# Group 1's first MLP product in seven half-size products, its weight sums read where GpSimd writes them

## The chip, the core and the metric

The kernel runs on one core of a Trainium2 chip. Five engines work side by side, each through its own instructions in order: TensorE (PE in the profile; PEld is its weight load), VectorE (DVE), ScalarE (ACT), GpSimd (POOL) and SyncE (SP), which here only issues DMAs. They wait for one another through semaphores. The metric is the device time of one execution in microseconds. All data are float32.

## The reference

Eight batches of 576 tokens go through chunked attention (8 heads of 64, chunks of 64 tokens), then a real two-dimensional Fourier mix over tokens and channels, a normalization, and an MLP with a residual. What matters here is the MLP, 512 to 2048 to 512:

```python
u = x + mixed
un = (u - mu) / np.sqrt(var + 1e-06)
ch = np.maximum(un @ w_ch1, 0.0) @ w_ch2
return (u + ch)
```

## The kernel before

**Groups.** Tokens are handled in tiles of 128. A tile LO or HI holds two chunks of one batch; a tile RE (rest) holds the middle chunks of two batches. Batch b's four LO and HI tiles are MLP group b (512 tokens), and the four rests are group 8: nine groups. `mlp(g)` (L1403) is a generator that issues the first product ("up") and the second ("down") of one group, and yields after each small piece.

**The step counter t.** The loop at L1484 counts these yields: t. After each, it issues side work: attention and Fourier mix of the next batch (`side`, spread evenly between due times `ready_at`), the preparation of the weights, and prefetches. So the order on every engine's queue is the order in which the program says it. `begin[g]` is the t at which group g starts; `begin[1]` is 32. Each up takes 16 steps; a down of group 0 takes 16, too, one for each m (128 of the 2048 hidden channels).

**Two forms of a product.** The plain form of up, `up_plain` (L1189), does for each m four matmuls of 128x128 weights by 512 tokens, and one ReLU by ScalarE from PSUM. In the profile each float32 matmul is two records. The other form, `up_halves` (L1245), splits weights, tokens and channels in halves and uses seven products of half size in place of eight (the Strassen-Winograd scheme). It goes over four pairs of m; a pair has seven turns, in the order `UP`, with four matmuls of 256 columns in each (r = 0, 1; kk = 0, 1). Its operands on the token side are the quarters of `unT`, the normalized and transposed tokens, and three sums of them, t1, t2, t4, with one quarter replaced, all made by `combined(g, q_)` (L1009) on VectorE. Its operands on the weight side are quarters of w_ch1 and four sums of them. The products gather in two PSUM tiles for each r, `pa` and `pb`, which take all four buffers of `ps_f`. Between products ScalarE copies one (L1267), VectorE adds five times for each m (L1268, L1270, L1272, L1278, L1281), and ScalarE applies the ReLU (L1276, L1279, L1282). A PSUM half is written again only after these have read it.

**Which group has which form.** `first_of = {1: 2, 2: 1}`: up is plain for groups 0 and 1, in halves from group 2; down is plain for group 0, in halves from group 1 (`down_halves`, L1291). For the last group down has a third form.

**Weights.** `wa` holds w_ch1 (`w1`), `wb` holds w_ch2 (`w2`). While group 0 runs, all weight pieces are rounded into place. `keep2` (GpSimd) makes the sums for down and SP stores them to DRAM (`s2`); this ends at t=31. `keep1` makes the sums for up during group 1, in four parts: GpSimd writes the sums to `yall` and to `os_` (the end of `wb`), and SP stores seven blocks for each part to DRAM (`s1`), 28 stores of 256 KB in all, in bunches of seven. Once `w1` is no more needed, `wa` becomes ten slabs that `fetch(1)` fills from `s1`; `wb` becomes three slabs of 1 MB that `fetch(2)` fills from `s2`, all three issued at t = begin[1] + 8.

**Around the start of group 1.** In the last steps of group 0's down, `turned(1, j)` (L997) transposes tile j on TensorE after m = 11 to 14, ScalarE copies the result to `unT` (L1007). After m=15, VectorE adds the residual to the four outputs (L1229) and the stores of group 0 go to SP and ScalarE (L1027, L1036). Beside it the attention of batch 2 runs: for each tile SP loads q and k (L250) and v (L273), VectorE transposes q and k (L416; for LO tiles GpSimd then copies a column, L418), TensorE makes scores (L448), transposes (L397) and the product with v (L498). `xall` keeps the attention outputs, 12 rows for tiles that rotate, 4 for the rests. GpSimd moves single token rows between tiles (L555) and folds the tiles for the Fourier mix (L570 to L595).

Of the kernel before, what the change touches and what calls it, by code (L numbers as in the profile page):

```python
# [11 lines left out]
ALU = mybir.AluOpType  # L12
# [4 lines left out]
def kernel(  # L17
# [32 lines left out]
    nc = tc.nc  # L50
    B, H, S, D = q.shape
    DM = H * D
    DFF = w_ch1.shape[1]
# [4 lines left out]
    NP = B // 2  # L58
    NJ = H // 2
    KD = DM // 128  # L60
    KF = DFF // 128
# [33 lines left out]
    wb = const.tile([128, KF * DM], FP32, name="wb")  # L95
    w1 = wa.rearrange("p (k f) -> p k f", k=KD)
# [6 lines left out]
    NO, HF = 7, KF // 2  # L103
    UP = (1, 0, 2, 3, 4, 6, 5)
    s1 = dram.tile([HF // 2, NO, 128, 2 * 2 * 128], FP32, name="s1")
    s2 = dram.tile([NO, 128, HF * HM], FP32, name="s2")
    NS1, NS2, Z1, Z2 = 10, 3, 2 * 2 * 128, HF * HM
    slab1 = [wa[:, i * Z1:(i + 1) * Z1].rearrange("p (k r f) -> p k r f", r=2, k=2) for i in range(NS1)]
    slab2 = [wb[:, i * Z2:(i + 1) * Z2].rearrange("p (m e) -> p m e", m=HF) for i in range(NS2)]
    tt = wa[:, NS1 * Z1:NS1 * Z1 + 3 * 2 * 256].rearrange("p (o k t) -> p o k t", o=3, k=2)  # L110
    tmp = wa[:, NS1 * Z1 + 3 * 2 * 256:NS1 * Z1 + 3 * 2 * 256 + 4 * 256].rearrange("p (i j t) -> p i j t", i=2, j=2)
    xs = wb[:, NS2 * Z2:NS2 * Z2 + HF * 256].rearrange("p (m t) -> p m t", m=HF)
    os_ = xs.rearrange("p (a b) t -> p a (b t)", b=2)
    yall = const.tile([128, 4, 512], FP32, name="yall")
# [66 lines left out]
    NG = len(groups)  # L181
# [3 lines left out]
    NR = 3 * G  # L185
    xall = const.tile([128, NR + NP, XW], FP32, name="xall")
# [819 lines left out]
        else:  # L1006
            nc.scalar.copy(unT[:, :, s * 128:(s + 1) * 128], pt)  # L1007

    def combined(g, q_):  # L1009

        unT = unTs[g]
        cl, ch = slice(q_ * 128, (q_ + 1) * 128), slice(256 + q_ * 128, 256 + (q_ + 1) * 128)
        b11, b12, b21, b22 = unT[:, 0:2, cl], unT[:, 0:2, ch], unT[:, 2:4, cl], unT[:, 2:4, ch]
        t1, t2, t4 = (tt[:, o, :, cl] for o in range(3))
        nc.vector.tensor_tensor(out=t1, in0=b12, in1=b11, op=ALU.subtract)
        nc.vector.tensor_tensor(out=t2, in0=b22, in1=t1, op=ALU.subtract)
        nc.vector.tensor_tensor(out=b12, in0=b22, in1=b12, op=ALU.subtract)
        nc.vector.tensor_tensor(out=t4, in0=b21, in1=t2, op=ALU.subtract)

    def store(n, o):  # L1020

# [14 lines left out]
                    eng.dma_start(out=out[b, t0 + 1 - r:t0 + CH:2, :], in_=o[r0 + ODD * r:r0 + ODD * r + ODD])  # L1036


    def keep1(i):

        f, kk = divmod(i, 2)
        lo, hi = slice(f * 512, (f + 1) * 512), slice(DFF // 2 + f * 512, DFF // 2 + (f + 1) * 512)
        a11, a12, a21, a22 = w1[:, kk, lo], w1[:, 2 + kk, lo], w1[:, kk, hi], w1[:, 2 + kk, hi]
        o1, o2, o3, o4 = ((os_ if i % 2 else yall)[:, j] for j in range(4))
        for out_, in0, in1, op in (
            (o1, a21, a22, ALU.add), (o2, o1, a11, ALU.subtract),
            (o3, a11, a21, ALU.subtract), (o4, a12, o2, ALU.subtract),
        ):
            nc.gpsimd.tensor_tensor(out=out_, in0=in0, in1=in1, op=op)
            yield  # L1050
        to = s1.rearrange("a o p (k x) -> p a o k x", k=2)[:, 2 * f:2 * f + 2]
        for o, a in enumerate((a11, o2, o1, o3, a12, o4, a22)):
            nc.sync.dma_start(out=to[:, :, o, kk], in_=a.rearrange("p (a x) -> p a x", a=2))
        yield

    def keep2(i):

# [23 lines left out]
    def block_of(name):  # L1081

        if name[0] == "s":
            return s3[STORED.index(name)]
        o, k = (2, "dw".index(name)) if name in "dw" else ({"b1": 0, "b2": 0, "b3": 4 + "12".index(name[2]), "b4": 4 + "12".index(name[2])}[name[:2]], (int(name[1]) - 1) % 2)
        return s2[o, :, k * Z3:(k + 1) * Z3]
# [38 lines left out]
                    yield  # L1125

    FEW = NG - 1
    first_of = {1: 2, 2: 1}
    n_slab = {1: 0, 2: 0, 3: 0}

    def fetch(which):
        i = n_slab[which]
        if which == 1 and i < HF // 2 * NO * (NG - first_of[1]):
            pair, o = divmod(i % (HF // 2 * NO), NO)
            nc.sync.dma_start(out=slab1[i % NS1].rearrange("p k r f -> p (k r f)"), in_=s1[pair, UP[o]])
        elif which == 3 and i < NR2 * (NG - FEW):
            to = slab3[i % NS3].rearrange("p m e -> p (m e)")
            nc.sync.dma_start(out=to, in_=block_of(PRODUCTS[i % NR2][1]))
        elif which == 2 and i < NO * (FEW - first_of[2]):
            nc.sync.dma_start(out=slab2[i % NS2].rearrange("p m e -> p (m e)"), in_=s2[i % NO])  # L1140
        n_slab[which] = i + 1

    lo, hi = slice(0, 256), slice(256, 512)
# [99 lines left out]


    def up_halves(g):  # L1245
        unT = unTs.pop(g)
        h1 = one_p.tile([128, KF, G * 128], FP32, tag="big", name="h1")
        rhs = (unT[:, 0:2, lo], tt[:, 1], tt[:, 0], unT[:, 0:2, hi], unT[:, 2:4, lo], unT[:, 2:4, hi], tt[:, 2])
        for pair in range(HF // 2):
            pas, pbs = {}, {}  # L1250
            for turn_, o in enumerate(UP):
                w = slab1[((g - first_of[1]) * HF // 2 * NO + pair * NO + turn_) % NS1]
                for r in range(2):
                    m = 2 * pair + r
                    a, b = tmp[:, r, 0], tmp[:, r, 1]
                    if o == 0:
                        pas[r] = ps_f.tile([128, 2, 256], FP32, tag="ff", name="pa")
                    if o == 1:
                        pbs[r] = ps_f.tile([128, 2, 256], FP32, tag="ff", name="pb")
                    dst = (pas, pbs, pas, pbs, pas, pas, pbs)[o][r][:, (0, 0, 1, 1, 0, 1, 1)[o]]  # L1260
                    for kk in range(2):
                        nc.tensor.matmul(  # L1262
                            out=dst, lhsT=w[:, kk, r], rhs=rhs[o][:, kk],
                            start=(o in (0, 1) and kk == 0), stop=(kk == 1), skip_group_check=True,
                        )
                    if o == 0:
                        nc.scalar.copy(a, dst)  # L1267
                        nc.vector.tensor_tensor(out=b, in0=pbs[r][:, 0], in1=a, op=ALU.add)  # L1268
                    elif o == 2:
                        nc.vector.tensor_tensor(out=a, in0=dst, in1=b, op=ALU.add)  # L1270
                    elif o == 3:
                        nc.vector.tensor_tensor(out=h1[:, HF + m, hi], in0=dst, in1=a, op=ALU.add)  # L1272
                        if pair > 0 and g < FEW:
                            operands(h1, m - 2)
                    elif o == 4:
                        nc.scalar.activation(out=h1[:, m, lo], in_=dst, func=ACTF.Relu)  # L1276
                    elif o == 5:
                        nc.vector.tensor_tensor(out=h1[:, m, hi], in0=dst, in1=b, op=ALU.add)  # L1278
                        nc.scalar.activation(out=h1[:, m, hi], in_=h1[:, m, hi], func=ACTF.Relu)  # L1279
                    elif o == 6:  # L1280
                        nc.vector.tensor_tensor(out=h1[:, HF + m, lo], in0=dst, in1=b, op=ALU.add)  # L1281
                        nc.scalar.activation(out=h1[:, HF + m], in_=h1[:, HF + m], func=ACTF.Relu)  # L1282
                fetch(1)
                if pair == HF // 4 and turn_ > 0 and g >= FEW:
                    sums(h1, EARLY.split()[turn_ - 1:turn_])
                if turn_ in (1, 3, 5, 6):
                    yield h1
        for m in (HF - 2, HF - 1) if g < FEW else ():
            operands(h1, m)
# [119 lines left out]
    with tc.manual_schedule():  # L1409
# [60 lines left out]
        begin = [0]  # L1470
# [1 line left out]
            begin.append(begin[-1] + (KF if g < first_of[1] else 2 * HF) + (KF if g < first_of[2] else 2 * NO if g < FEW else NR2 // 2))  # L1472
        ready_at = [begin[g] + (2 * KF - 7 if g < first_of[2] else 2 * HF + 4) for g in range(NG)]
        conv2 = iter([step for i in range(HF // 2) for step in [keep2(i ^ 1)]])
        conv1 = iter([step for i in range(4) for step in [keep1(i)]])

        def chain(gens):
            for gen in gens:
                yield from gen

        n_whole, late, rest_ = 0, [], None
        conv2, conv1 = chain(conv2), chain(conv1)
        t = 0
        for g in range(NG):  # L1484
            for _ in mlp(g):
# [4 lines left out]
                late = []  # L1490
                if t == 8:
                    nc.scalar.copy(tk, early_tk[:, :, :, 0:NE])
                if cur < len(sides):
                    t0 = 3 if cur == 0 else ready_at[cur - 1]
                    t1 = ready_at[cur]
# [19 lines left out]
                if t == begin[1] - 1:  # L1515
                    for _ in conv2:
                        pass
                if t == ready_at[NG - 3]:
                    rest_ = make_rest()
                    next(rest_)  # L1520
# [5 lines left out]
                    slab3.extend(a.rearrange("p (m e) -> p m e", m=4) for a in more)  # L1526
                if begin[FEW] + 2 <= t < begin[FEW] + 2 + NS3:
                    fetch(3)
                if begin[1] <= t < begin[1] + KF // 2:
                    for _ in range(3):  # L1530
                        next(conv1, None)
                if t == begin[1] + KF // 2:
                    for _ in range(NS2):
                        fetch(2)
                if t == begin[1] + KF:
                    for _ in range(NS1):
                        fetch(1)
# [49 lines left out]
```

## Time and profile before

| | |
|---|---|
| median of 3 runs | 1076.75 us (1076.54 to 1077.28) |
| the profiled execution | 1076.13 us |
| its span, first to last instruction | 1074.1 us |
| granted TensorE clock, mean | 0.997 |
| instructions | 19924 |
| group 1 up, 16 m | 190.49 to 255.96 us |
| group 1 down | 255.96 to 314.17 us |
| group 2 up, 28 turns | 314.17 to 370.13 us |
| DMA engines busy, 190 to 255 us | 0.77, 243 GB/s |

The span is the part of the execution that the trace covers; some 2 us lie around it. Busy time of TensorE is modelled from the instructions, so a share near 1 says that it has no gaps and not that it works at its peak. A time of a record is longer than its pace, since records overlap: the pace is read from the chain of waits, where a piece of work counts until the next one takes over. In answers of the trace, a bracket behind an instruction tells how long its engine was idle before it and what ended that.

### The profile page before, as it was taken

Reading aid. Unit: us, or ns where it says so; the run is one execution under the profiler, and the core shown is the slowest. Engines: PE = TensorE matmul, PEld = TensorE weight load, DVE = VectorE, ACT = ScalarE, POOL = GpSimd, SP = SyncE. Lnnn points to the kernel's source line nnn. Section 1 sums busy time; section 2 is a strip of 40 time slices with the busy share of each in tenths; the row PEclk is TensorE's granted clock in tenths of the full one; section 3 lists DMA queues with packets and bytes.
Section 4 is the critical chain, followed back from the end, with each engine's and each line's share of the span. In section 5 each row is a group of like instructions: output and inputs, shape, how many; then the busy total and the mean of one; then the engine's idle time right before and its main releaser. Section 6 shows DMA issues by size and latency. Waiting matters only on the chain.

```text
span 1074.1 us, 19924 instructions
## 1 busy us (share of the span) xinstructions
PE 1052.4 (98%) x7402; PEld 838.0 (78%) x7402; DVE 586.5 (55%) x1271; ACT 310.6 (29%) x730; POOL 406.8 (38%) x531
## 2 busy tenths in 40 slices
PE   8899989999999999999999999999999999999997
PEld 6645444446888888888888888888888888888886
DVE  4798985324556455655565555745664535433331
ACT  4688563122113410323022312331134103101200
POOL 4310018483514240254124321525151726780281
PEclk9999999999999999999999999999999999999999
DMA  8677566598468635892678356954653659776763
GB/s 171 215 204 217 126 196 189 176 295 287 155 182 238 173 134 179 235 253 91 194 214 239 119 166 190 258 159 154 208 174 107 222 188 334 244 233 190 280 229 104
DMA packets 159293, 212.71 MB, mean 198 GB/s; under 512 B 69308, under 2 KB 106172, under 8 KB 152926
## 3 DMA queue, kind: packets, MB, share of 16 engines
q1 hardware_dynamic: 155548, 208.04, 62.6%
q10 hardware_dynamic: 3330, 2.76, 1.1%
q8 instruction: 59, 0.97, 0.4%
q0 software_dynamic: 320, 0.66, 0.3%
q14 instruction: 36, 0.29, 0.1%
HBM read 177.31 MB, written 34.08 MB: 197 GB/s over the span
## 4 chain that ended last, share of the span: by engine, by line
PE 82%; DMA 5%; DVE 5%; ACT 3%; SPq 3%; issue 1%; POOL 0%; DVEq 0%; ACTq 0%
PE pb L1313 18%; PE pa L1262 18%; PE pa L1313 14%; PE pb L1262 13%; PE dn L1377 4%; PE up L1195 4%; PE pt L397 2%; PE dn L1216 2%; DMA xall<-in_moe_w_ch_dram 2%; PE mix L838 2%; PE z L719 1%; PE xp L498 1%; PE sc L448 1%; SPq L263 1%; DMA out_dram<-o 1%
## 5 line engine op out<-in xcount | busy, mean ns | idle before, releaser
L1262 PE MATMUL pa<-unT,wa 128*128 128x256 f32 x672 | 160.0, 381 | 1.5 <-DVE wa L1270 1.5
L1262 PEld LDWEIGHTS pa<-unT,wa 128*128 128x128 f32 x672 | 126.3, 190 | 19.3 <-DVE wa L1270 2.0
L1262 PE MATMUL pb<-wa 128*128 128x256 f32 x448 | 106.6, 381 | 0.0
L1313 PE MATMUL pa<-wb,h 128*128 128x256 f32 x448 | 101.6, 380 | 0.0
L1313 PE MATMUL pb<-wb,h 128*128 128x256 f32 x448 | 100.8, 380 | 0.0
L1262 PEld LDWEIGHTS pb<-wa 128*128 128x128 f32 x448 | 84.4, 190 | 11.5
L1313 PEld LDWEIGHTS pa<-wb,h 128*128 128x128 f32 x448 | 83.9, 190 | 11.2
L1313 PEld LDWEIGHTS pb<-wb,h 128*128 128x128 f32 x448 | 84.1, 190 | 10.9
L1149 POOL TENSOR_TENSOR h<-h 128x256 f32<-128x256 f32 x56 | 47.7, 861 | 98.7 <-DVE wb L1147 95.4
L555 POOL COPY xall<-xall 1x512 f32<-1x512 f32 x28 | 17.8, 636 | 147.9 <-DVE xall L515 120.4
L1268 DVE TENSOR_TENSOR wa<-pb,wa 128x256 f32<-128x256 f32 x56 | 23.8, 424 | 69.9 <-ACT wa L1267 69.9
L1216 PE MATMUL dn<-wb,h 128*128 128x512 f32 x128 | 59.2, 611 | 0.0
L1195 PE MATMUL up<-unT,wa 128*128 128x512 f32 x128 | 56.8, 596 | 0.0
L1267 ACT COPY wa<-pa 128x256 f32<-128x256 f32 x56 | 20.9, 373 | 123.8 <-PE pa L1262 98.9
L1262 PE MATMUL pa<-wa 128*128 128x256 f32 x224 | 53.9, 383 | 0.0
L1262 PE MATMUL pb<-unT,wa 128*128 128x256 f32 x224 | 52.9, 379 | 0.0
L1313 PE MATMUL pb<-wb,yall 128*128 128x256 f32 x224 | 51.2, 382 | 0.0
L1313 PE MATMUL pb<-wb 128*128 128x256 f32 x224 | 50.7, 379 | 0.0
L1313 PE MATMUL pa<-wb,yall 128*128 128x256 f32 x224 | 50.5, 379 | 0.0
L1276 ACT ACTIVATE h<-pa 128x256 f32<-128x256 f32 x56 | 21.5, 384 | 99.3 <-PE pa L1262 98.3
L1175 PE MATMUL up<-unT,wa 128*128 128x512 f32 x108 | 49.4, 598 | 0.0
L855 POOL TENSOR_TENSOR xall<-y,xall 128x513 f32<-128x513 f32 x14 | 21.4, 1526 | 68.4 <-DVE y L849 68.4
(287 smaller groups left out, 1977.9 us busy)
## 6 DMA issues: line engine op xcount, KB each, us to landing
wb<-s SPq DMA_DIRECT2D x49, 1024.0 KB
wa<-s SPq DMA_DIRECT2D x196, 256.0 KB
xall<-in_moe_w_ch_dram SPq DMA_DIRECT2D x22, 512.0 KB
q<-in_q_dram SPq DMA_DIRECT2D x96, 112.0 KB
k<-in_k_dram SPq DMA_DIRECT2D x96, 112.0 KB
wb<-s SPq DMA_DIRECT2D x16, 512.0 KB
v<-in_v_dram SPq DMA_DIRECT2D x124, 64.0 KB
s<-part SPq DMA_DIRECT2D x30, 256.0 KB
```

The lines of the kernel that those rows point to most:

```text
L397: nc.tensor.transpose(pt[:, j, :], src(j), ident)
L838: nc.tensor.matmul(out=mix[:, cols], lhsT=zt[:, T], rhs=tab, start=(T == 0), stop=(T == 3), skip_group_check=True,)
L855: eng.tensor_tensor(out=x[:, 0:w], in0=y[:, 0:w], in1=x[:, 0:w], op=ALU.add)
L1149: nc.gpsimd.tensor_tensor(out=h1[:, m, hi], in0=h1[:, m, lo], in1=h1[:, m, hi], op=ALU.subtract)
L1175: nc.tensor.matmul(out=up, lhsT=w1[:, kk, m * 128:(m + 1) * 128], rhs=unT[:, kk], start=(kk == 0), stop=(kk == KD - 1), skip_group_check=True,
L1195: nc.tensor.matmul(out=up, lhsT=w1[:, kk, m * 128:(m + 1) * 128], rhs=unT[:, kk], start=(kk == 0), stop=(kk == KD - 1),)
L1216: nc.tensor.matmul(out=dn, lhsT=h1[:, m, s * 128:(s + 1) * 128], rhs=w2[:, m, :], start=(m == 0), stop=(m == KF - 1),)
L1262: nc.tensor.matmul(out=dst, lhsT=w[:, kk, r], rhs=rhs[o][:, kk], start=(o in (0, 1) and kk == 0), stop=(kk == 1), skip_group_check=True,)
L1268: nc.vector.tensor_tensor(out=b, in0=pbs[r][:, 0], in1=a, op=ALU.add)
L1276: nc.scalar.activation(out=h1[:, m, lo], in_=dst, func=ACTF.Relu)
L1313: nc.tensor.matmul(out=dst, lhsT=lhs[:, m], rhs=w[:, m], start=(o in (0, 2) and m == 0), stop=(m == HF - 1), skip_group_check=True,)
L1377: nc.tensor.matmul(out=dst, lhsT=lhs[:, m], rhs=w[:, m], start=(fresh and not half and m == 0), stop=(m == 3), skip_group_check=True,)
```

## The change

Group 1's up takes the form in halves. Its weights are not fetched from DRAM but read in place: quarters from `w1`, the sums where GpSimd writes them, which is now the front of `wb` (12 blocks of 512 columns, `made1`), but for one sum that replaces a quarter of `w1`. `keep1` makes the four sums of one whole pair at t = 31, 33, 35 and 37, without a DMA; the 28 stores follow one by one, two for each step from t=33 to 46 (`keep1_store`). The three slabs of `w2` are fetched at begin[1] + 9, + 13 and + 16, one each.

Group 1's t1, t2, t4 and the two temporaries of the recombination can't lie in `wa`, where `w1` still is. They go to rows of `xall`: t1 and t2 to the rests' last two rows, which are not yet filled, t4 and the temporaries to group 0's rows. Since group 0's outputs are added from these rows, t4 is made later: `combined(1, q_)` without it runs in the steps of m=13 and m=14, and the two missing subtractions are issued at the start of `up_halves`. The arithmetic of group 1 thus changes its order of summation; nothing else is computed differently.

```diff
+    tt_1 = [rest_rows[:, i * 512:(i + 1) * 512].rearrange("p (k t) -> p k t", k=2) for i in range(2)]
+    tt_1.append(gone_rows[:, 1024:1536].rearrange("p (k t) -> p k t", k=2))
+    tmp_1 = gone_rows[:, 0:1024].rearrange("p (i j t) -> p i j t", i=2, j=2)
+
+    def combined(g, q_, late=False):
...
+        t1, t2, t4 = (tt_1[o][:, :, cl] if g == 1 else tt[:, o, :, cl] for o in range(3))
+        if late:
+            nc.vector.tensor_tensor(out=t4, in0=b21, in1=t2, op=ALU.subtract)
+            return
         nc.vector.tensor_tensor(out=t1, in0=b12, in1=b11, op=ALU.subtract)
         nc.vector.tensor_tensor(out=t2, in0=b22, in1=t1, op=ALU.subtract)
         nc.vector.tensor_tensor(out=b12, in0=b22, in1=b12, op=ALU.subtract)
-        nc.vector.tensor_tensor(out=t4, in0=b21, in1=t2, op=ALU.subtract)
+        if g > 1:
+            nc.vector.tensor_tensor(out=t4, in0=b21, in1=t2, op=ALU.subtract)
...
+    def made1(pair, j):
+        return wb[:, (3 * pair + j) * 512:(3 * pair + j + 1) * 512].rearrange("p (k x) -> p k x", k=2)
+
+    def parts1(pair):
+        a11, a12, a21, a22 = w1_part(pair, 0, 0), w1_part(pair, 0, 2), w1_part(pair, 1, 0), w1_part(pair, 1, 2)
+        o1, o2, o4 = (made1(pair, j) for j in range(3))
+        return a11, o2, o1, a21, a12, o4, a22
+
+    def keep1(pair):
+
+        a11, o2, o1, a21, a12, o4, a22 = parts1(pair)
         for out_, in0, in1, op in (
             (o1, a21, a22, ALU.add), (o2, o1, a11, ALU.subtract),
-            (o3, a11, a21, ALU.subtract), (o4, a12, o2, ALU.subtract),
+            (a21, a11, a21, ALU.subtract), (o4, a12, o2, ALU.subtract),
         ):
             nc.gpsimd.tensor_tensor(out=out_, in0=in0, in1=in1, op=op)
-            yield
...
+    def keep1_store(i):
+        pair, o = i // NO, (2, 1, 5, 3, 0, 4, 6)[i % NO]
+        to = s1[pair, o].rearrange("p (k x) -> p k x", k=2)
+        nc.sync.dma_start(out=to, in_=parts1(pair)[o])
...
-    first_of = {1: 2, 2: 1}
+    first_of = {1: 1, 2: 1}
...
     def up_halves(g):
+        if g == 1:
+            combined(1, 0, True)
+            combined(1, 1, True)
...
+                if g == 1:
+                    w = parts1(pair)[o].rearrange("p k (r f) -> p k r f", r=2)
+                else:
+                    w = slab1[((g - 2) * HF // 2 * NO + pair * NO + turn_) % NS1]
...
+                if begin[1] - 1 <= t < begin[1] + 7 and t % 2:
+                    keep1((t - begin[1] + 1) // 2)
...
-                if begin[1] <= t < begin[1] + KF // 2:
-                    for _ in range(3):
-                        next(conv1, None)
-                if t == begin[1] + KF // 2:
-                    for _ in range(NS2):
-                        fetch(2)
+                if begin[1] < t < begin[1] + KF:
+                    for i in range(2):
+                        if n_kept < HF // 2 * NO:
+                            keep1_store(n_kept)
+                            n_kept += 1
+                if t in (begin[1] + 9, begin[1] + 13, begin[1] + 16):
+                    fetch(2)
```

The loop's calls of `keep1` and `keep1_store` stand behind the side work of the same step.

More of the change, by code (lines that the diff above doesn't have):

```diff
@@ L1007, in turned @@
             nc.scalar.copy(unT[:, :, s * 128:(s + 1) * 128], pt)
-    def combined(g, q_):
+    rest_rows = xall[:, NR + NP - 2:NR + NP, :].rearrange("p a f -> p (a f)")
+    gone_rows = xall[:, 0:4, :].rearrange("p a f -> p (a f)")
+    tt_1 = [rest_rows[:, i * 512:(i + 1) * 512].rearrange("p (k t) -> p k t", k=2) for i in range(2)]
+    tt_1.append(gone_rows[:, 1024:1536].rearrange("p (k t) -> p k t", k=2))
+    tmp_1 = gone_rows[:, 0:1024].rearrange("p (i j t) -> p i j t", i=2, j=2)
+    def combined(g, q_, late=False):
         unT = unTs[g]
@@ L1013, in combined @@
         b11, b12, b21, b22 = unT[:, 0:2, cl], unT[:, 0:2, ch], unT[:, 2:4, cl], unT[:, 2:4, ch]
-        t1, t2, t4 = (tt[:, o, :, cl] for o in range(3))
+        t1, t2, t4 = (tt_1[o][:, :, cl] if g == 1 else tt[:, o, :, cl] for o in range(3))
+        if late:
+            nc.vector.tensor_tensor(out=t4, in0=b21, in1=t2, op=ALU.subtract)
+            return
         nc.vector.tensor_tensor(out=t1, in0=b12, in1=b11, op=ALU.subtract)
@@ L1036, in store, with w1_part @@
                     eng.dma_start(out=out[b, t0 + 1 - r:t0 + CH:2, :], in_=o[r0 + ODD * r:r0 + ODD * r + ODD])
[L1039 to L1044, printed above, removed]
+    def w1_part(pair, side, k0):
+        c0 = side * (DFF // 2) + pair * 256
+        return w1[:, k0:k0 + 2, c0:c0 + 256]
+    def made1(pair, j):
[6 more added lines that the diff above has]
+        a11, o2, o1, a21, a12, o4, a22 = parts1(pair)
         for out_, in0, in1, op in (
             (o1, a21, a22, ALU.add), (o2, o1, a11, ALU.subtract),
-            (o3, a11, a21, ALU.subtract), (o4, a12, o2, ALU.subtract),
+            (a21, a11, a21, ALU.subtract), (o4, a12, o2, ALU.subtract),
         ):
             nc.gpsimd.tensor_tensor(out=out_, in0=in0, in1=in1, op=op)
-            yield
[L1051 to L1054, printed above, removed]
+    def keep1_store(i):
+        pair, o = i // NO, (2, 1, 5, 3, 0, 4, 6)[i % NO]
+        to = s1[pair, o].rearrange("p (k x) -> p k x", k=2)
+        nc.sync.dma_start(out=to, in_=parts1(pair)[o])
     def keep2(i):
@@ L1132, in fetch @@
         i = n_slab[which]
-        if which == 1 and i < HF // 2 * NO * (NG - first_of[1]):
+        if which == 1 and i < HF // 2 * NO * (NG - 2):
             pair, o = divmod(i % (HF // 2 * NO), NO)
@@ L1245, in up_halves @@
     def up_halves(g):
+        if g == 1:
+            combined(1, 0, True)
+            combined(1, 1, True)
         unT = unTs.pop(g)
         h1 = one_p.tile([128, KF, G * 128], FP32, tag="big", name="h1")
-        rhs = (unT[:, 0:2, lo], tt[:, 1], tt[:, 0], unT[:, 0:2, hi], unT[:, 2:4, lo], unT[:, 2:4, hi], tt[:, 2])
+        t1, t2, t4 = tt_1 if g == 1 else (tt[:, o] for o in range(3))
+        rhs = (unT[:, 0:2, lo], t2, t1, unT[:, 0:2, hi], unT[:, 2:4, lo], unT[:, 2:4, hi], t4)
         for pair in range(HF // 2):
@@ L1251, in up_halves @@
             for turn_, o in enumerate(UP):
-                w = slab1[((g - first_of[1]) * HF // 2 * NO + pair * NO + turn_) % NS1]
+                if g == 1:
+                    w = parts1(pair)[o].rearrange("p k (r f) -> p k r f", r=2)
+                else:
+                    w = slab1[((g - 2) * HF // 2 * NO + pair * NO + turn_) % NS1]
                 for r in range(2):
                     m = 2 * pair + r
-                    a, b = tmp[:, r, 0], tmp[:, r, 1]
+                    a, b = (tmp_1 if g == 1 else tmp)[:, r, 0], (tmp_1 if g == 1 else tmp)[:, r, 1]
                     if o == 0:
@@ L1282, in up_halves @@
                         nc.scalar.activation(out=h1[:, HF + m], in_=h1[:, HF + m], func=ACTF.Relu)
-                fetch(1)
+                if g > 1:
+                    fetch(1)
                 if pair == HF // 4 and turn_ > 0 and g >= FEW:
@@ L1474 @@
         conv2 = iter([step for i in range(HF // 2) for step in [keep2(i ^ 1)]])
-        conv1 = iter([step for i in range(4) for step in [keep1(i)]])
         def chain(gens):
@@ L1479, in chain @@
                 yield from gen
-        n_whole, late, rest_ = 0, [], None
-        conv2, conv1 = chain(conv2), chain(conv1)
+        n_whole, n_kept, late, rest_ = 0, 0, [], None
+        conv2 = chain(conv2)
         t = 0
```

## The prediction

> **What bounds the kernel now.** I read the busy table and the chain of waits first, then a table of busy time by stage, then the chain and the timeline of the one stage that is edited. The first two lines are of the page; the next two are stages from the table by windows (start:end, length, then busy time of PE, PE's weight loads, VectorE, ScalarE, GpSimd).
>
> ```profile
> PE 1052.4 (98%) x7402; PEld 838.0 (78%) x7402; DVE 586.5 (55%) x1271; ACT 310.6 (29%) x730; POOL 406.8 (38%) x531
> PE 82%; DMA 5%; DVE 5%; ACT 3%; SPq 3%; issue 1%; POOL 0%; DVEq 0%; ACTq 0%
> ...
> 190.00:255.00 65.00, 63.29 (x403) 30.39 (x405) 26.18 (x50) 13.03 (x23) 43.20 (x59) 1.00 0.77 243
> 314.00:370.00 56.00, 56.00 (x483) 48.25 (x474) 33.07 (x76) 17.37 (x42) 20.27 (x38) 1.00 0.74 213
> ```
>
> TensorE sets the end. The first window is group 1's first product in plain form, the second is group 2's in seven half-size products. TensorE is idle for 1.71 us of the first and never in the second. So TensorE time saved in the first window is worth its full size, unless a wait takes it back. The chain (start, length, what) gives the unit prices and the one wait that is there already:
>
> ```profile
> 195.56 8.46 DMA out_dram<-o
> ...
> 204.89 6.17 DMA k<-in_k_dram
> ...
> 211.18 1.09 DVE kT L416
> ...
> 212.33 0.69 PE sc L448 x32
> 213.02 10.50 PE up L1195 x24
> ...
> 319.62 1.73 PE pb L1262 x8
> ```
>
> Twenty-four records of 512 columns take 10.5 us here, and pieces of eight take 3.44 elsewhere in this stage: 3.44 us for one m (4 matmuls, each two records). Eight records of 256 columns take 1.73: one turn (a product for both r). Above that stands a chain that is not TensorE's: the output stores of group 0 hold the issue of a k load, the k tile lands at 211.06, VectorE transposes it (L416), and only then the scores (L448) may start. The timeline around the stage's start (start, length, engine, line) shows who is early and who is late there:
>
> ```profile
> 185.18 1.10 DVE L416 STREAM_TRANSPOSE qT<-q 128x512 f32<-128x512 f32 x1
> 186.41 0.20 POOL L418 COPY qT<-qT 128x8 f32<-128x8 f32 x1 [0.33 <-DVE qT L416]
> 187.05 3.60 PE L1216 MATMUL dn<-wb,h 128*128 128x512 f32 x8
> 187.25 0.59 ACT L1007 COPY unT<-pt 128x512 f32<-128x512 f32 x1 [5.31 <-PE pt L397]
> 188.19 0.69 DVE L1229 TENSOR_TENSOR o<-dn,xall 128x512 f32<-128x512 f32 x1 [1.90 <-PE dn L1216]
> ...
> 211.18 1.09 DVE L416 STREAM_TRANSPOSE kT<-k 128x512 f32<-128x512 f32 x1 [8.93 <-DMA k<-in_k_dram]
> ```
>
> **What the Trainium skill says.** "PSUM — Partial Sum Buffer", section Engine vs sequencer instructions: the queues of ScalarE, VectorE and GpSimd are strict FIFO, and matmuls start in program order. The trace agrees: VectorE sat 8.93 us behind one k transpose. The same page, section PSUM bank collisions, wants accesses guarded by bank, not by address; pa and pb hold two halves in one bank, so a product waits for the reader of the other half. "SBUF — State Buffer", section Who interferes with whom: a VectorE instruction with two SBUF inputs contends with GpSimd's reads, one with at most one does not. The trace agrees: L1148 took 0.43 us alone and 0.88 at 248 us beside GpSimd, while L1281, which reads PSUM, stayed within 0.400 to 0.428 in all 56.
>
> **The change, part by part.**
>
> *TensorE.* Removed: 16 m x 3.44 = 55.0 us. Added: 28 turns x 1.727 = 48.4. Net -6.7. The transposes, scores and other side work in the stage (65.5 - 55.0 - 1.7 = 8.8 us) stay, and the steps t are 16 as before.
>
> *The sums GpSimd makes.* 16 instructions of 1.27 us stay 16 (L1049 becomes the new keep1), but pair 0's are now due at once: the first turn takes o2, the second sum. They are put at t=31, behind the qT copy L418 of the same step. And combined(1, 1), now in the m=14 step, goes on VectorE ahead of that step's qT transpose. It needs the ScalarE copy L1007, which ends at 187.84. So: three additions of about 0.48 (L1015 to L1017) to 189.3; qT to 190.4; L418 to 190.7; two sums to 193.25. TensorE ends L1216 at 190.65 and waits about 2.65 us. VectorE's four L1229 slip to 193.2 as well; they free the banks at 191.1, 191.8, 192.5 and 193.2, earlier than a start at 193.3 needs them. The other sums have slack: pair 1 is made by about 201 and wanted at 207; pair 3 stands behind the row shift (L555, 3.9 us, after about 214.3), is made by 223.5 and wanted at about 234.
>
> *The wait for k.* Counting from 193.3: nine turns (15.5), two transposes, two attention products and one score (2.6) bring TensorE to the score of the fourth tile at 211.4. Nothing edited stands before that k load on SP: the new stores come behind it in t=33 and q waits for no later qT than 190.4, against its issue at 191.5. So k lands at 211.06 again and the score starts at 212.3. **The wait at the start is hidden**: without it TensorE would stand 3.4 us here, with it 0.9. The price is that what the first nine turns save (5 x 3.44 - 15.5 = 1.7) is lost here.
>
> *From 213.0 on.* Left before: 11 m = 37.8 us; left after: 19 turns = 32.8. **Gain 5.0 us.**
>
> *VectorE.* Added: 40 recombinations x 0.42 = 16.8 and combined, 8 x 0.47 = 3.8, so 26.2 rises to about 46.8 of 60 us. Group 2's stage carries 33.1 of 56 without a stall. But before, ScalarE alone emptied PSUM here; now L1268 to L1281 stand on VectorE behind each L416 that waits for a load. In group 2's stage the reads end some 2 us before the bank is rewritten (L1272 at 320.94, the next write at 322.91), so a longer block stops TensorE. When do loads land after 213? SP issues without a pause from 212 to 241. Before, seven stores stood ahead of a k load; now two per step. With its own durations (0.5 a store, 2.0 for q or k, 2.8 for v) from 210: fourth tile's successor q issued by 215.9, k by 219.1, next q by 226.2, k by 230.5; landing about 2.5 us after (L250 ended 223.9, transposed 226.54), so at 218.4, 221.7, 228.7, 233. VectorE gets there at about 219, 222.5, 229, 233.5. It fits by half a microsecond each; cost taken 0, bounds 0 to +4.6 (next but one paragraph). GpSimd beside L1147 and L1148 adds up to 0.45 each, inside the 2 us.
>
> *ScalarE.* 16 ReLUs of 0.60 go, 32 instructions (0.37, 0.38, 0.42, 0.63) come: +4.8 us on 13.0, hidden.
>
> *DMA.* 28 stores of 256 KB as before; the three slabs of w2 go out at +9, +13 and +16 instead of all at +8. The third may start only when TensorE leaves pair 3; it is wanted two products of 6.9 us and some z work later, over 15 us. A 1 MB slab stands for 8.99 us once in the chain, at 660. Hidden by about 6 us. The ten slabs of w1 keep their place.
>
> Sum, from the profiled execution: 1076.13 - 5.0 = 1071.1 us (span 1074.1 to 1069.1, 2.0 around it). The median shown is 0.6 above that execution, so **1071.7**. All later stages are full with TensorE (59.0 of 59, 56.0 of 56), so nothing there absorbs it.
>
> **Rivals.**
>
> *The k load slips too.* If group 0's stores, whose inputs come up to 2 us later, push the k load by those 2 us, the score starts at 214.3: gain 3.0, 1073.7. For it: the chain runs through those stores. Against: SP reaches the first at 194.9, and the last L1229 ends at 193.2.
>
> *VectorE's queue takes the gain back (slower).* At the k transposes of the fifth and sixth tile the recombinations are held. If these loads land where they did before (226.5, 242.3), the score waits 1.4 us, and pair 3's second turn, which needs the bank that L1278 empties behind the transpose, about 3.2: together 4.6, gain 0.4, 1076.3, no change. From there each microsecond later is lost; with both 2 us later it is 3.6 us slower, **1080.3**. For it: DMA engines are busy 0.92 of 215 to 256, and margins are 0.5 us. Against: fewer stores stand ahead of each load, and group 2's stage, with the same orders, shows no such wait.
>
> *All of it comes.* If k lands before 210, the score starts at 211.4: gain 5.9, 1070.8. Nothing in the diff moves that load.
>
> *It does not do what it says.* first_of[1]=1 sends group 1 through up_halves, and its weights are parts1: no chance given.
>
> **How the numbers follow.** The likeliest (0.58, own range 1070.6 to 1073.2), all of it (0.05), k slips (0.14): faster 0.77. VectorE's queue to a draw 0.09, to slower 0.14. What a measurement can tell is about 0.2%, 2.2 us, so faster means under 1074.6. The range reaches from 1069.8 (0.9 under 1071.7 with one more us for the landing) to 1076.0; what is left out is the slower case and part of the draw, 0.19.
>
> **What would show it.** Right: 224 records of 256 columns in group 1's first product, eight in 1.73 us; the first one at about 193.3, released by GpSimd; the fourth tile's score at 212.3 again; the first down product near 251.0 instead of 256.0; idle of L416 after 213 under 1 us each; 58.2 us from there to group 2's first product as before. Wrong: TensorE idle behind L1268 to L1281, a k load landing after 213, a wait of the third w2 slab, or a start at 190.7 (then GpSimd's order was misread).

## The result, and the profile after

| | before | after |
|---|---|---|
| median of 6 runs, us | 1076.96 (1075.29 to 1078.53) | 1073.76 (1072.44 to 1074.69) |
| the profiled execution, us | 1076.13 | 1074.23 |
| its span, us | 1074.1 | 1072.2 |
| instructions | 19924 | 20212 |

The ratio is 0.9971 [0.9958, 0.9983]: the kernel is 3.2 us faster, where 5.0 were forecast. When it was measured again beside the experiments (14 runs against 19 of the kernel before), the ratio was 0.9972 [0.9963, 0.9981].

The page's busy line and its chain by engine, after:

```profile
PE 1046.3 (98%) x7498; PEld 854.6 (80%) x7498; DVE 610.8 (57%) x1319; ACT 315.3 (29%) x746; POOL 406.6 (38%) x531
PE 77%; DVE 8%; DMA 5%; ACT 4%; SPq 3%; issue 2%; POOL 1%; DVEq 0%; ACTq 0%; POOLq 0%
```

TensorE is busy 6.1 us less (1052.4 to 1046.3; 6.7 were worked out). But its share of the chain fell from 82 to 77%, and VectorE's rose from 5 to 8%: some of what was saved has become waiting. The same table by windows as before shows in which stage:

```profile
190.00:255.00 65.00, 61.05 (x542) 51.47 (x542) 46.36 (x95) 17.93 (x40) 44.47 (x61) 1.00 0.68 205
314.00:370.00 56.00, 56.00 (x467) 48.27 (x466) 33.61 (x76) 18.82 (x46) 19.03 (x37) 1.00 0.72 212
```

TensorE now stands still for 3.95 of the 65 us (1.71 before). Group 2's stage still has no gap. VectorE carries 46.36 us of this window; 46.8 were worked out for the stage.

The timeline around the stage's start and up to the score of the fourth tile (start, length, engine, line; in brackets the idle time before it and what ended that):

```profile
188.39 0.42 DVE L1026 TENSOR_TENSOR unT<-unT 128x256 f32<-128x256 f32 x1
188.73 1.11 DVE L416 STREAM_TRANSPOSE qT<-q 128x512 f32<-128x512 f32 x1
...
189.97 0.20 POOL L418 COPY qT<-qT 128x8 f32<-128x8 f32 x1 [3.72 <-DVE qT L416]
190.12 1.27 POOL L1069 TENSOR_TENSOR wb<-wa 128x512 f32<-128x512 f32 x1
191.47 1.26 POOL L1069 TENSOR_TENSOR wb<-wb,wa 128x512 f32<-128x512 f32 x1
...
192.78 1.99 PE L1289 MATMUL pb<-xall,wb 128*128 128x256 f32 x8 [2.41 <-POOL wb L1069]
...
211.13 1.09 DVE L416 STREAM_TRANSPOSE kT<-k 128x512 f32<-128x512 f32 x1 [3.74 <-DMA k<-in_k_dram]
...
212.28 0.70 PE L448 MATMUL sc<-kT,qT 64*64 64x64 f32 x32 [0.70 <-DVE kT L416]
```

This is the order that the prediction read: combined(1, 1) ahead of qT, qT ahead of the GpSimd copy L418, two sums of `keep1` (now L1069), and only then the first product. TensorE waits 2.41 us. The score starts at 212.28, as before. What is new lies behind it, on VectorE and GpSimd:

```profile
216.13 1.27 POOL L1069 TENSOR_TENSOR wb<-wa 128x512 f32<-128x512 f32 x1
216.21 1.47 DVE L1167 TENSOR_TENSOR wb<-h 128x256 f32<-128x256 f32 x1
217.48 1.33 POOL L1069 TENSOR_TENSOR wb<-wb,wa 128x512 f32<-128x512 f32 x1
217.71 1.37 DVE L1168 TENSOR_TENSOR yall<-wb,h 128x256 f32<-128x256 f32 x1
...
218.19 1.03 PE L1289 MATMUL pb<-xall,wa 128*128 128x256 f32 x4
...
219.34 1.15 DVE L1167 TENSOR_TENSOR wb<-h 128x256 f32<-128x256 f32 x1
219.48 1.13 PE L1289 MATMUL pb<-xall,wa 128*128 128x256 f32 x4 [0.26 <-DVE h L1299]
220.53 1.37 DVE L1168 TENSOR_TENSOR yall<-wb,h 128x256 f32<-128x256 f32 x1
...
223.35 1.97 PE L1289 MATMUL pb<-xall,wb 128*128 128x256 f32 x8 [0.58 <-DVE h L1308]
...
225.15 1.89 PE L1289 MATMUL pa<-unT,wa 128*128 128x256 f32 x8
...
231.31 0.41 DVE L1167 TENSOR_TENSOR wb<-h 128x256 f32<-128x256 f32 x1
```

L1167 and L1168 (L1147 and L1148 before) make the sums that down needs. Alone one takes 0.41 us (last line). Beside the four sums of keep1(3) each takes 1.15 to 1.47 us. The PSUM readers behind them in VectorE's queue (L1299, L1308) come late, and TensorE stops twice, for 0.26 and 0.58 us. These waits count from the end of a record, which lies later than the pace of the work. By the starts of the turns the two stops cost more: from 218.19 to 225.15 pass 6.96 us, for three turns (1.73 each) and one transposition (0.44), which make 5.62 without a stop. That is 1.34 us lost.

**Where the 3.2 us come from.** Three lengths divide the profiled executions: the edited stage (start of the last record of group 0's down to group 1's first down product), group 1's down (to group 2's first product), and what follows (to the first product of the last down).

| us | before | after | after, again |
|---|---|---|---|
| edited stage | 65.9 | 62.5 | 62.5 |
| group 1's down | 58.2 | 58.7 | 58.2 |
| what follows | 709.2 | 710.5 | 710.6 |

The edited stage gives 3.4 us. In the first profile of the kernel after, 0.5 are given back in the next stage and 1.3 in what follows, so the two profiled executions differ by 1.9 us and not by the 3.2 of the medians. Of the 1.3, 1.0 is waiting: TensorE's waits in what follows took 2.5 us in place of 1.5 (one stop at 671 us, where VectorE waits for a q load). Over all ten profiles these waits took 1.5 to 3.4 us, in kernels with and without the change, and the row 709.2 to 713.1, so nothing here ties the 1.3 us to the change.

### The profile page after: what moved, and what is told of

It is laid out like the page before. It is cut to its first block, busy times and chain, and to the rows that moved or that the text cites. A ratio compares the mean times of both kernels' runs of the same rounds, so it can differ in the third digit from the quotient of the medians.

```text
span 1072.2 us, 20212 instructions
## 1 busy us (share of the span) xinstructions
PE 1046.3 (98%) x7498; PEld 854.6 (80%) x7498; DVE 610.8 (57%) x1319; ACT 315.3 (29%) x746; POOL 406.6 (38%) x531
## 4 chain that ended last, share of the span: by engine, by line
PE 77%; DVE 8%; DMA 5%; ACT 4%; SPq 3%; issue 2%; POOL 1%; DVEq 0%; ACTq 0%; POOLq 0%
PE pa L1289 19%; PE pb L1341 18%; PE pb L1289 14%; PE pa L1341 13%; PE dn L1405 4%; PE pt L397 2%; PE mix L838 2%; DMA xall<-in_moe_w_ch_dram 1%; SPq L263 1%; PE xp L498 1%; PE z L719 1%; DVE power L378 1%; DMA out_dram<-o 1%; PE sc L448 1%; DMA v<-in_v_dram 1%
## 5 line engine op out<-in xcount | busy, mean ns | idle before, releaser
L1289 PE MATMUL pa<-unT,wa 128*128 128x256 f32 x736 | 175.0, 381 | 2.5 <-DVE wa L1297 2.5
L1289 PEld LDWEIGHTS pa<-unT,wa 128*128 128x128 f32 x736 | 138.3, 190 | 21.8 <-DVE wa L1297 2.7
L1289 PE MATMUL pb<-wa 128*128 128x256 f32 x448 | 106.9, 381 | 0.1
L1289 PEld LDWEIGHTS pb<-wa 128*128 128x128 f32 x448 | 84.1, 190 | 12.3 <-DVE h L1299 0.5
L1289 PE MATMUL pb<-unT,wa 128*128 128x256 f32 x256 | 60.5, 379 | 0.0
L1303 ACT ACTIVATE h<-pa 128x256 f32<-128x256 f32 x64 | 24.6, 384 | 114.1 <-PE pa L1289 113.6
L1294 ACT COPY wa<-pa 128x256 f32<-128x256 f32 x56 | 20.9, 372 | 123.5 <-PE pa L1289 80.6
L1289 PEld LDWEIGHTS pb<-unT,wa 128*128 128x128 f32 x256 | 48.6, 190 | 6.6
L1289 PE MATMUL pa<-wa 128*128 128x256 f32 x224 | 53.9, 383 | 0.0
L1309 ACT ACTIVATE h<-h 128x512 f32<-128x512 f32 x64 | 39.6, 629 | 45.0 <-DVE h L1308 44.8
L1195 PE MATMUL up<-unT,wa 128*128 128x512 f32 x108 | 49.4, 598 | 0.0
```

Source lines behind the costliest of these rows:

```text
L1195: nc.tensor.matmul(out=up, lhsT=w1[:, kk, m * 128:(m + 1) * 128], rhs=unT[:, kk], start=(kk == 0), stop=(kk == KD - 1), skip_group_check=True,
L1289: nc.tensor.matmul(out=dst, lhsT=w[:, kk, r], rhs=rhs[o][:, kk], start=(o in (0, 1) and kk == 0), stop=(kk == 1), skip_group_check=True,)
```

## The experiments

Theory going in: the start wait is real but hidden behind the k load; the shortfall comes from GpSimd slowing VectorE. Rivals: the start wait is what costs, or a queue of loads. Where no number of runs is given, a kernel was executed once, so the length of its edited stage ("stage" below) is read rather than its total; the kernel before took 1076.8 us beside the first four.

**Sums for pair 0 one step sooner.** On the kernel after:

```diff
-                if t == begin[1] - 1:
+                if t == begin[1] - 2:
...
+                    keep1(0)
-                if begin[1] - 1 <= t < begin[1] + 7 and t % 2:
+                if begin[1] <= t < begin[1] + 7 and t % 2:
```

> The changed kernel, with pair 0's four sums issued one step earlier (t=30), ahead of the qT copy that held them. Places in the changed kernel's trace: first product starts at 192.78 us, the fourth tile's score at 212.28, first down product at 252.29. Theory (the start wait is hidden by the k load): the first product starts at about 190.4 and the 2.41 us wait for GpSimd is gone, but the score still starts at 212.0 to 212.6, with its wait up from 0.7 to about 3 us, and the first down product stays at 252.0 to 252.6. Rival (the start wait is part of the gain that is missing): the score starts near 210 and the first down product near 249.9.

Measured: 1077.29 us, stage 67.2. Neither side had this. The timeline of that kernel:

```profile
187.19 1.27 POOL L1069 TENSOR_TENSOR wb<-wb,wa 128x512 f32<-128x512 f32 x1
187.26 1.48 DVE L1024 TENSOR_TENSOR xall<-unT 128x256 f32<-128x256 f32 x1
188.41 1.46 POOL L1069 TENSOR_TENSOR wa<-wa 128x512 f32<-128x512 f32 x1
188.78 1.37 DVE L1025 TENSOR_TENSOR xall<-unT,xall 128x256 f32<-128x256 f32 x1
...
190.08 1.48 DVE L1026 TENSOR_TENSOR unT<-unT 128x256 f32<-128x256 f32 x1
191.48 1.09 DVE L416 STREAM_TRANSPOSE qT<-q 128x512 f32<-128x512 f32 x1
...
193.24 3.52 PE L1289 MATMUL pb<-xall,wb 128*128 128x256 f32 x8 [3.19 <-DVE o L1249]
```

GpSimd was early, but its sums now ran beside combined(1, 1), whose three additions took 1.37 to 1.48 us instead of 0.42. qT and the bank-freeing L1249 slipped by 2.8 us; TensorE waited 3.19 us, now for VectorE, and q's load on SP, which waits for qT, pushed k with it (2.3 us of wait at the score). So in the kernel after the sums behind L418 are not only late, they are also out of VectorE's way. And the first turn took 3.52 us instead of 1.99: after each of the two gaps the granted clock was lower, 0.87 and 0.70 from 190 to 198 us, 0.86 and 0.71 from 214 to 222.

**The fourth tile's k ahead of group 0's stores.** Its buffer was the one that q and k loads rotate through; it gets a place of its own, free by then, so that it can be issued behind its q:

```diff
+                if n == at[HI, 2, 0] and nm == "k":
+                    t = yall.rearrange("p a b -> p (a b)")[:, 1024:2048].rearrange("p (j x) -> p j x", j=NJ)
+                else:
+                    t = one_p.tile([128, NJ, 4 * D], FP32, tag=nm, name=nm)
...
+            if n + 1 == at[HI, 2, 0]:
+                which = "qk" if which == "q" else ""
```

> The changed kernel, with the fourth tile's k loaded into an unused half of yall, issued right behind its q and so ahead of group 0's output stores. Theory (the stores ahead of it on SP and in the DMA queues make k late): k is there before 207, VectorE does not wait for it, the score starts at 211.4 to 211.8 (its place in TensorE's order behind the start wait of 2.4), the first down product at about 251.6, so 0.7 us gained and no more. Rival (the loads behind it become late instead): VectorE waits for the fifth tile's q or k by a microsecond or more, and the first down product stays at 252.3 or later.

Measured: 1075.35 us, stage 63.2. The timeline of TensorE (L1294 is L1289 of the kernel after), then two rows of the table by windows, whose last three columns are granted clock, DMA share and GB/s:

```profile
192.03 3.35 PE L1294 MATMUL pb<-xall,wb 128*128 128x256 f32 x8 [2.41 <-POOL wb L1074]
195.17 2.26 PE L1294 MATMUL pa<-unT,wa 128*128 128x256 f32 x8
...
212.33 0.64 PE L453 MATMUL sc<-kT,qT 64*64 64x64 f32 x32
```

```profile
190.00:194.00 4.00, 1.97 (x6) 1.59 (x7) 3.63 (x5) 0.00 (x0) 3.92 (x4) 0.81 0.46 124
194.00:198.00 4.00, 4.00 (x18) 3.35 (x17) 0.54 (x2) 0.78 (x3) 3.92 (x4) 0.76 0.66 178
```

The score has no wait left: the transpose of k had ended 3.0 us before it. VectorE waits for none of the loads behind it either, so the delay that the rival had expected did not come. But the stage is not shorter: the same start gap of 2.41 us was this time followed by a clock of 0.81 and 0.76, and the first two turns took 1.4 and 0.4 us more. In the two profiles of the kernel after, and in the next run, the same 2.41 us brought no such dip. The length alone would have said that the k load costs nothing; the two readings together say that its gain was eaten at the start.

**All sums of keep1 before the first L1167.** In steps 31, 32, 33 and 34 in place of 31, 33, 35 and 37:

```diff
-                if begin[1] - 1 <= t < begin[1] + 7 and t % 2:
-                    keep1((t - begin[1] + 1) // 2)
+                if begin[1] - 1 <= t < begin[1] + 3:
+                    keep1(t - begin[1] + 1)
```

> The changed kernel, with the sums of pairs 0 to 3 issued at t = 31, 32, 33, 34 instead of 31, 33, 35, 37, so that pair 3's are made before the row shift and before pair 1's operands. Theory (VectorE's additions with two SBUF inputs are held by GpSimd's sums, and this costs TensorE the two waits of 0.26 and 0.58 us at 219 and 223): the four additions L1167 and L1168 of pair 1 fall from 1.15 to 1.47 us each to 0.4 to 0.9, both waits vanish, and the first down product comes about 0.8 us sooner, 251.3 to 251.7. Rival (VectorE is late there because of its load of work or of a q transpose): the waits stay within 0.2 us of what they were.

Measured: 1074.2 us, stage 61.8. The timeline of VectorE:

```profile
217.46 0.41 DVE L1167 TENSOR_TENSOR wb<-h 128x256 f32<-128x256 f32 x1
217.90 0.42 DVE L1168 TENSOR_TENSOR yall<-wb,h 128x256 f32<-128x256 f32 x1
...
218.58 0.61 DVE L1167 TENSOR_TENSOR wb<-h 128x256 f32<-128x256 f32 x1
219.23 0.42 DVE L1168 TENSOR_TENSOR yall<-wb,h 128x256 f32<-128x256 f32 x1
```

The four additions are back at 0.41 to 0.61 us, and both waits (0.26 and 0.58) are gone. TensorE over the same turns that took from 218.19 to 225.15 in the kernel after:

```profile
219.44 1.89 PE L1289 MATMUL pb<-xall,wa 128*128 128x256 f32 x8
...
222.89 0.60 PE L397 MATMUL pt<-ident,ex 128*128 128x128 f32 x4
223.33 1.89 PE L1289 MATMUL pb<-xall,wb 128*128 128x256 f32 x8
225.06 1.89 PE L1289 MATMUL pa<-unT,wa 128*128 128x256 f32 x8
```

They take 5.62 us here in place of 6.96. The stage is only 0.7 shorter than the 62.5 of after, because the k load came 0.7 later after the start of the stage, which the edit does not explain, and the score waited 1.4 (the start wait was still 2.41). So the first down product, at 252.2, missed the expected 251.3 to 251.7. From the start of the score to the first down product the edit is worth its full size:

| us, from the fourth tile's score to the first down product | |
|---|---|
| before | 43.6 |
| after, in both profiles, and the three other variants with the sums at t = 31, 33, 35, 37 | 39.9 to 40.0 |
| this run, and the last version below, with the same sums | 38.7 and 38.6 |

This shows the cause: GpSimd's instructions are all that the edit moves, and the loss goes with them, with the late k and without it.

**The same k load in the kernel before**, placed in rows of `xall` that are free there.

> The kernel before, with the fourth tile's k loaded sooner, as in e2, into two rows of xall that are not used yet. Theory: its one wait of 1.71 us at the score (212.32) goes, the score starts at about 210.6, and the first down product moves from 255.96 to about 254.3. Rival (the moved load only delays another): the first down product stays within 0.4 us of 255.96.

Measured: 1081.93 us, stage 65.2. The wait of 1.71 us at that score is gone, but the next tile's score waits 1.0 instead, so only 0.7 of it comes through. So neither side is right in full. The total says nothing of the edit: the stretch ahead of the stage was 2.6 us longer than before and what follows 3.9, in places that the edit doesn't touch. In what follows, TensorE waited 3.4 us in place of 1.5, and behind one of these waits, of 2.3 us at 451, the granted clock fell to 0.55 to 0.59 for 4 us. It was run once.

**Pair 0 without the start wait.** Turns 0 and 1 of group 1's first pair are exchanged, so that the first product takes a quarter of `w1` and the sum is wanted one turn later:

```diff
+            swapped = g == 1 and pair == 0
-            for turn_, o in enumerate(UP):
+            for turn_, o in enumerate((0, 1, 2, 3, 4, 6, 5) if swapped else UP):
...
-                    if o == 0:
+                    if o == (1 if swapped else 0):
                         nc.vector.tensor_tensor(out=b, in0=pbs[r][:, 0], in1=a, op=ALU.add)
```

> The changed kernel, with the first two turns of pair 0 exchanged for group 1: the product with a11, which needs no sum, comes first, so that nothing is moved on GpSimd. Measured from the start of group 0's last product record to group 1's first down product, the kernel before took 65.9 us and the changed one 62.5. Theory (the k load sets the score, so the start wait is hidden): TensorE's gap at the start falls from 2.4 to at most 0.5 us, with 0.5 to 1.0 before the second turn, but the score's wait for k rises from 0.7 to about 2.4 us, and the length stays at 62.1 to 62.9. Rival (the start wait costs its size): 60.8 or less.

Measured: 1075.79 us, stage 61.5. TensorE's waits from 186 to 330 us (what waited, for what, us in total, times, longest):

```profile
PE sc L448 <- DVE kT L416: 1.4, 1, 1.4
PE pb L1290 <- DVE h L1310: 0.6, 1, 0.6
PE pb L1290 <- POOL wb L1069: 0.4, 1, 0.4
PE pb L1290 <- DVE h L1301: 0.3, 1, 0.3
```

The 2.41 became 0.4, and the score's wait grew from 0.7 only to 1.4, not to the 2.4 that full cover would give. So of the 2.0 us taken away at the start about 1.0 came through (62.5 to 61.5), between theory and rival. In this run the k load came 1.0 sooner after the start of the stage: on SP, the q load ahead of it waited 1.3 us for group 0's stores in place of 3.2. Why these stores landed sooner is not shown, and the run with the sums sooner, whose k came 0.7 later with nothing changed at the start, says how far this load wanders. The 1.0 is one profile, and its size is rough. The total is no shorter than that of after because the stretch ahead of the stage was 3.9 us longer, where the edit touches nothing.

**Both**, the exchanged turns and the sooner k:

> As f1_swap, and the fourth tile's k loaded sooner as in e2. Theory: with both waits gone the length falls to 59.9 to 60.5 us (1.7 from the start and 0.7 from the score), the two waits of 0.26 and 0.58 us beside GpSimd's sums remain. Rival (what the loads give, a later load takes): 61.5 or more, with VectorE waiting for a later q or k.

Measured: 1071.67 us, stage 59.8. Of TensorE's waits only 0.4 (GpSimd), 0.6 and 0.2 (the two behind L1167 and L1168) are left. With the start gap gone the clock stayed at full, and the k edit, which by itself had shown nothing in the length, is worth 1.7 us (61.5 to 59.8), of which the score's wait was 1.4.

**All of it**: these two, the sums in steps 31 to 34, and the second slab of w2 issued at begin[1] + 12 ahead of that step's side work.

```diff
+                if t == begin[1] + 12:
+                    fetch(2)
...
-                if t in (begin[1] + 9, begin[1] + 13, begin[1] + 16):
+                if t in (begin[1] + 9, begin[1] + 16):
```

> As f2_swap_k, with the sums of pairs 0 to 3 at t = 31 to 34 as in e4, and the second slab of w2 fetched at begin[1] + 12, ahead of that step's side loads. Theory: all four waits named so far are gone, the length is 59.0 to 59.8 us, group 1's down takes 58.2 us again, and the time is 6.5 us under the kernel before: 1070 to 1071, ratio 0.994. Rival (SP falls further behind the faster TensorE, so the slabs of w2 come late): group 1's down grows by 1 us or more, and the ratio stays at 0.996 or above.

Measured in 6 runs: median 1070.16 us (1067.61 to 1071.18), ratio to the kernel before 0.993 [0.9912, 0.9949], stage 58.5. Its waits from 186 to 330 us, and its edited stage by windows:

```profile
PE pb L1348 <- DMA wb<-s: 0.8, 1, 0.8
PE pb L1295 <- POOL wb L1074: 0.4, 1, 0.4
```

```profile
190.00:255.00 65.00, 64.59 (x591) 53.96 (x590) 45.45 (x96) 18.58 (x43) 44.53 (x61) 1.00 0.73 223
```

TensorE stands still for 0.41 of the 65 us, where the kernel after had 3.95. The stage is shorter than the expected 59.0 to 59.8. But its earlier end makes the third slab late (0.8 us), and group 1's down took 59.0 and not the expected 58.2: of the rival, that much is true. This version is the fastest of all that ran: 6.9 us under the kernel before, 4.0 under the kernel after (measured side by side: 1077.07 and 1074.15).

The kernel after, run again beside these:

> The changed kernel unchanged, beside the others on one chip. Theory: 3.2 us under the kernel before (ratio 0.9971), 62.5 us for the length; from run to run the times differ by some 2 us, since the clock of TensorE dips after its start wait of 2.4 us in some runs and not in others. Rival: the length differs between runs by 0.3 us at most, and the spread comes from elsewhere.

Measured: median 1074.15 us of 14 runs (1072.25 to 1075.46), stage 62.5, and the same four waits in the stage (2.4, 0.7, 0.6, 0.3), with no dip of the clock in it. That the spread from run to run comes from dips after the start wait is not supported: the kernel before, which has no such wait, spread over 5.5 us in 19 runs, this one over 3.2 in 14.

## Why the prediction was right, and where its size was off

The direction and the path were right; the gain was 3.2 us, not 5.0. The range was wide enough to hold that. The measured 1073.76 happens to lie on the 1073.7 of the rival in which k slips, but k did not slip; the loss came from a term that the prediction had taken as covered. By its own steps:

- **TensorE's work**, -6.7 us: its busy time fell by 6.1.
- **The start wait for GpSimd**, 2.65 us: 2.41, with the releaser and the queue order as worked out.
- **The score of the fourth tile** at 212.3: 212.28, with 0.70 us of wait where 0.9 was said. (The 3.4 us "without it" should read 3.55 by its own terms, 0.9 and 2.65.) "The wait at the start is hidden" holds for the comparison of before and after, since the score was not later. As a statement of what removing the wait would bring it is half right: about 1.0 of 2.0 us came through in the one run of the exchanged pair. It also ignored the clock, which the same gap lowered in one of four profiles. "TensorE: Matmul & The Clock Gate", section Why this matters for your kernels, of the Trainium skill, advises "No PE-idle gaps >~3µs between matmul bursts". The 3.19 us of the first experiment fit that; the dips after 2.41 us, and after the 2.29 at that experiment's score, show that a gap below it is not always safe.
- **From 213 on, gain 5.0**: 3.6 came (43.6 us from the score to the first down product before, 40.0 after). The shortfall of 1.4 is one mis-sized term: "GpSimd beside L1147 and L1148 adds up to 0.45 each, inside the 2 us". Beside a run of `keep1`'s sums it adds 0.74 to 1.06 each, four in a row. That is more than the 2 us of slack, and it costs TensorE 1.34 us. With the sums out of the way 38.7 us are left, a gain of 5.0, as forecast. It is not a matter of the late score: with k sooner and no wait there, the two stops were the same (0.6 and 0.2). Nor did it need an experiment to be seen. The term was sized by one row of the kernel before, 0.88 us at 248; two microseconds earlier the same timeline has a longer GpSimd instruction, and the addition beside it takes 1.37:

```profile
245.46 1.32 POOL L570 TENSOR_TENSOR sum<-xall 128x512 f32<-128x512 f32 x1 [0.19 <-DVE xall L515]
245.69 1.37 DVE L1148 TENSOR_TENSOR yall<-wb,h 128x256 f32<-128x256 f32 x1
```

  In this the prediction's first sign of being wrong, "TensorE idle behind L1268 to L1281", did come, in small: the two readers are L1272 and L1281 of the kernel before.
- **The loads after 213**, cost 0: right. VectorE waits for no load from 213 to the end of the stage (before: 5.75 us at the fifth tile's k), so the slower rival did not happen. The rival in which k slips by 2 us did not happen either.
- **The third slab of w2 hidden by 6 us**: it was the second that came late. SP reached it only at 254.77, behind the stores and loads of its queue. The chain of waits of the kernel after:

```profile
254.77 6.44 DMA wb<-s
261.35 3.69 PE pa L1341 x16
```

  TensorE waited 0.3 us, and group 1's down took 58.7 in place of 58.2 in one profile of the kernel after, 58.2 in the other.
- **The first down product** at 251.0: 252.29. **The medians**: 3.4 of the edited stage less 0 to 0.5 of the next agree with the 3.2 measured.

How often the clock dips in the executions that have no profile, and why the k load came 1.0 us sooner in one run and 0.7 later in another, stays open.

## What to carry to other kernels

Price a VectorE instruction with two inputs in SBUF at the length of the GpSimd instruction that may run beside it, not at its own, take it from the longest such row that the trace shows, and place GpSimd's work where VectorE has none of these. A wait that another wait covers is free only as long as the other stays: take away both, or the second takes over, and read a variant by its waits as well as by its length. When TensorE gets faster in one stage, look at once at the queue that has to supply the next.

## What was not expected of the hardware

- VectorE's addition of 128x256 floats with both inputs in SBUF took 0.41 us alone and up to 1.48 beside GpSimd's 128x512 sums of 1.27. In the timeline it ends about 0.28 us after the GpSimd instruction does (217.68 after 217.40, 219.08 after 218.81), so it is held until that one has ended; GpSimd's own sums rose to 1.45 at most in the kernel after. "SBUF — State Buffer", section Who interferes with whom, of the Trainium skill, names this pair as one that contends and calls the shared port an exclusive lock; the runs agree, and add the size.
- The granted clock fell to 0.81 and 0.76 (means over 4 us) after one gap of 2.41 us in TensorE's work, and stayed at 1.00 after three others of the same length. This dip cost some 1.7 us (two turns with 5.61 us of records against 3.88). It is not rare: the ten profiles hold 18 gaps of 2.06 to 2.96 us, and within 4 us behind 10 of them the clock fell, to 0.50 to 0.55 at its lowest (means over 2 us); it fell behind all three gaps of 3.19 to 3.44 us and behind none of the eight of 1.5 to 2.0. What decides in a single case is not shown.
